# Two 576 KB weight transfers issued ahead of a 4 MB one at the head of a DMA queue

## The chip, the cores and the metric

The kernel runs on one core of a Trainium2 chip. The metric is the device time of one execution in microseconds. The core has five engines with instruction streams of their own: TensorE (PE in the profile, its weight loads PEld), VectorE (DVE), ScalarE (ACT), GpSimd (POOL) and SyncE (SP), and 16 DMA engines that carry the transfers that SP and ACT issue.

## The reference

One decoding step of a block with two branches over the same normalized input. The batch is 4, the model width D is 576, and there is one token per sequence.

```python
def reference(A_x, A_k_cache, A_v_cache, A_wq, A_wo, B_x, B_w1, B_w2, B_w3, B_w4):
    x = A_x                                   # (4, 1, 576)
    xn = _layernorm(x, axis=-1)
    return x + _A_ref(xn, A_k_cache, A_v_cache, A_wq, A_wo) + _B_ref(xn, B_w1, B_w2, B_w3, B_w4)

# branch A: attention over the last W = 2048 cached positions, 32 query heads, 16 KV heads, head size 128
    q = (x @ wq) split into heads
    p = softmax(q k^T * Dh ** -0.5);  o = p v
    return o @ wo
# branch B: mixer and MLP
    h = gelu(layernorm(x) @ w1)               # w1: 576 x 576
    hs = concatenate([g0, g1, g2, g3]) @ w2   # four shifted quarters of h; w2: 576 x 576
    x1 = x + hs
    return x1 + gelu(layernorm(x1) @ w3) @ w4 # w3: 576 x 4608, w4: 4608 x 576
```

With one token per sequence the shifts along the sequence leave only zeros in the shifted quarters, so the product with w2 is taken of an array of zeros (`hs_inT`), as the kernel has it.

## The kernel before

All weights and the window of the caches are read once from device memory: 88.49 MB. Nearly all of it goes over SP's queue, as the list `prog["sp"]`, which is sorted by each transfer's key (line 638) and issued in that order. A transfer that has to wait for a semaphore holds up all that SP would issue behind it.

At the head of that queue stand the weights of the first stages, each cut in a main part (rows 0 to 511, four rows on each of 128 partitions) and a rest (rows 512 to 575, split in halves over 128 partitions, `rag_src`, line 209). The keys set the order: wq and its rest (-50 and -49, lines 274 and 275), w1 main and rest (-48, line 276), w2 main and rest (-47, line 277), w3 main and rest (-46, line 278), the first 24 row groups of w4 (-45, line 281), then the 16 blocks of the K cache of 2 MB (lines 295 to 297), the 8 of V of 4 MB (lines 298 to 301) with the rest of w4 among them, and wo in five pieces (lines 304 to 307). The input x is issued on ACT's queue (line 273). The main parts of wq, w1 and w2 take 4096, 576 and 576 KB; their rests take 512, 72 and 72 KB.

Some buffers are used twice, and this sets waits. The main part of wq lies in the third and fourth slot of the K ring (line 88), so the third K transfer waits until the query projection is done (`["q"]`, line 296); from the fifth on, a K transfer waits for the transposes of the block that had its slot. w1 and w2 lie in the first half of `ktb` (lines 102 to 105), which the K stage uses later.

TensorE works through its own list in order of keys: the transposes of the normalized x (`pe_xT`, lines 331 to 340), the query projection in five steps (`pe_q`, lines 364 to 376, matmuls on line 371), the transposes of q (line 384), the product with w1 (`pe_hh`, line 400, matmuls on line 405), the product with w2 in two halves (`pe_hs`, line 410, lines 413 and 414), the transpose of the third layer norm's result, three matmuls that set accumulators to zero (`pe_bank0`, line 359), the product with w3 (`pe_h2`, lines 445 and 451), and the first part of the product with w4 (`pe_MO`, line 398). Then come the 16 K blocks (transposes on line 507, scores on line 514), the softmax, the product with V (line 575) and the product with wo (line 398 again). VectorE runs the layer norms (`ln_ops`, line 314, its last step on line 324) and copies out of PSUM, also in order of keys: the copy of the transposed x for the projection (line 352) stands behind the second layer norm. GpSimd sets up masks and clears buffers, among them the second half of `ktb` (line 246).

A wait of an operation is written as a list of names; for a transfer, `add_dma` (line 198) returns the semaphore and the count to wait for. Each pair of a list given to `add_dma` is one transfer that adds 16 to that semaphore.

Of the kernel before, what the change touches and what calls it, by code (L numbers as in the profile page):

```python
# [37 lines left out]
def bass_parallel_sum__sliding_block_cached__mixer_s_mlp__decode_kernel(  # L38
# [32 lines left out]
    with ExitStack() as ctx:  # L71
        def sb(name, shape, dt):
            return ctx.enter_context(nc.sbuf_tensor(name, shape, dt))

        def sem(name):
            return ctx.enter_context(nc.semaphore(name))
# [21 lines left out]
        def cut(n):  # L98
            nonlocal _o
            _o += n  # L100
            return ktb[:, _o - n:_o]
        w1main = cut(4 * D).rearrange("p (r n) -> p r n", r=4)
        w1rag = cut(HALF)
        w2main = cut(4 * D).rearrange("p (r n) -> p r n", r=4)
        w2rag = cut(HALF)
# [23 lines left out]
        hs_inT = sb("hs_inT", [128, 6, B], BF16)  # L129
# [64 lines left out]
        def add(engine, emit, waits=(), sig=None, key=0.0, inc=None):  # L194
            seqc[0] += 1
            prog[engine].append(Op(emit, waits, sig, key, seqc[0], inc))

        def add_dma(pairs, skey, waits=(), key=0.0, engine="sp"):
            if skey not in S:
                S[skey] = sem("s_" + "_".join(str(k) for k in (skey if isinstance(skey, tuple) else (skey,))))  # L200
            dma_count[skey] = dma_count.get(skey, 0) + 16 * len(pairs)

            def emit(e):
                for o_, i_ in pairs:
                    e.dma_start(o_, i_).then_inc(S[skey], 16)
            add(engine, emit, waits, None, key)
            return ("dma", skey, dma_count[skey])

        def rag_src(w_ap):
            return w_ap[512:576, :].rearrange("r (h n) -> (r h) n", h=2)  # L210
# [46 lines left out]
        for gl in range(2):  # L257
            for x in range(2 * NVS):
# [3 lines left out]
                  waits=["pick11"], sig=f"pick2{gl}{x}", key=-84 + 0.1 * (8 * gl + x))  # L262


        def mask_of(t, tag, view):
# [7 lines left out]
        ev_x = add_dma([(x_sb[:], x2)], "x", (), -100, engine="act")  # L273
        ev_wq = [add_dma([(kring[:, 2 * UE:4 * UE], A_wq[0:512, :].rearrange("(p r) n -> p (r n)", r=4))], "wq", (), -50),
                 add_dma([(wqrag, rag_src(A_wq))], "wqr", (), -49)]
        ev_w1 = add_dma([(w1main, B_w1[0:512, :].rearrange("(p r) n -> p r n", r=4)), (w1rag, rag_src(B_w1))], "w1", (), -48)
        ev_w2 = add_dma([(w2main, B_w2[0:512, :].rearrange("(p r) n -> p r n", r=4)), (w2rag, rag_src(B_w2))], "w2", (), -47)
        ev_w3 = add_dma([(vring[:, 0:4 * F], B_w3[0:512, :].rearrange("(p r) n -> p (r n)", r=4)), (w3rag, rag_src(B_w3))],
                        "w3", (), -46)
        w4s = B_w4.rearrange("(p r) n -> p r n", r=W4R)  # L280
# [69 lines left out]
        for idx, (src, tag, dst) in enumerate(((xn_bf, "ln1", xnT), (xn2_bf, "ln2", xn2T))):  # L350
            add("pe", pe_xT(src, idx), waits=["ident_bf", tag], sig=f"xT{idx}", key=-50 + idx)
            add("dve", lambda e, dst=dst, idx=idx: e.tensor_copy(out=dst[:], in_=XTps[idx]), waits=[f"xT{idx}"], sig=f"xnT{idx}",  # L352
                key=-29 + idx * 0.1)
# [36 lines left out]
        for k in range(2):  # L390
            for g in range(2):
# [3 lines left out]
                    waits=["qTp1"], sig=f"qT{2 * k + g}", key=-10 + 0.1 * k)  # L395
# [4 lines left out]
        def pe_hh(e):  # L400
# [4 lines left out]
                    ins = e.matmul(HHps[h], lhsT=x_, rhs=w, start=(r == 0), stop=(r == 4), tile_position=(0, 32 * h),  # L405
                                   skip_group_check=True)
            return ins
        add("pe", pe_hh, waits=[ev_w1, "xnT1"], sig="hT", key=-24)

        def pe_hs(h):  # L410
            def f(e):
                for r in range(4):
                    e.matmul(HSps, lhsT=hs_inT[:, r, :], rhs=w2main[:, r, HALF * h:HALF * (h + 1)], start=(r == 0), stop=False)
                return e.matmul(HSps, lhsT=hs_inT[:, 4 + h, :], rhs=w2rag, start=False, stop=True)
            return f
        for h in range(2):
            cs = slice(HALF * h, HALF * (h + 1))
            add("pe", pe_hs(h), waits=[ev_w2, "hs_inT"] + (["x1a"] if h else []), sig=f"hs{h}", key=-23 + h)
            add("dve", lambda e, cs=cs: e.tensor_tensor(out=x1_bf[:, cs], in0=HSps, in1=xn_bf[:, cs], op=ALU.add),
                waits=[f"hs{h}"], sig="x1" if h else "x1a", key=-7 + 0.1 * h)  # L420
        ln_ops(2, x1_bf, x1n_bf, ["x1"], "ln3", -6)
# [3 lines left out]
            waits=["hT", "ln3_sd"], sig="gelu_h", key=-5.9)  # L425
# [38 lines left out]
        for k in range(3):  # L464
            add("pe", pe_h2(k), waits=[ev_w3] + (["x1nT", "gelu_h", "h2_zero"] if k == 0 else []), sig=f"h2_{k}", key=-18 + k)
            add("act", lambda e, k=k: e.activation(out=h2_sb[:, k], in_=H2ps[k], func=ACTF.Gelu_apprx_tanh), waits=[f"h2_{k}"],
                sig=f"gelu2_{k}", key=-5 + 0.1 * k)
# [3 lines left out]
            waits=["h2Tp"], sig="h2T", key=-4.5)  # L471
# [16 lines left out]
        def evac(n):  # L488
            if n % 8 in ACT_EVAC:
                return "act", lambda e: e.activation(out=ktbuf[:, n % NKT], in_=tb[n % 4], func=ACTF.Copy)  # L490
            return "dve", lambda e: e.tensor_copy(out=ktbuf[:, n % NKT], in_=tb[n % 4])  # L491

        for n in range(NB):
            c, k = n // NBLK, n % NBLK
            if k == 0:
                add("dve", lambda e, c=c: e.tensor_copy(out=Qs[:, c % N_CB, :], in_=Qpad_t[:, 128 * (4 * CH[c][0] + CH[c][1]):][:, 0:128]),
                    waits=[f"SC{c - 2}"] if c >= 1 else ["qT3"], key=n)
            eng, f = evac(n)
# [11 lines left out]
        def emit_SC(e, k):  # L510
# [11 lines left out]
            waits=["rmax"], sig="negb", key=KS + 0.05)  # L522
        for q in range(4):
            add("act", lambda e, q=q: e.activation(out=P_sb[:, q, :], in_=Sps[:, q, :], func=ACTF.Exp,
                                                   bias=negb[:, 0:1], scale=scale, accum_out=rs4[:, q:q + 1]),
                waits=["negb"], sig=f"exp{q}", key=KS + 0.1 + 0.01 * q)
# [16 lines left out]
        for qt in range(4):  # L543
            k0 = KS + 0.9 + 0.1 * qt
            add("pe2", pe_PT(qt), waits=[f"PTx{q}" for q in range(4)] + (["pick217"] + [f"E{NB - 1 - k}" for k in range(4)] if qt == 0 else []),
                sig=f"PTp{qt}", key=k0)
            if qt % 2 == 1:
                add("dve", lambda e, qt=qt: e.tensor_copy(out=PT_t[:, 512 * qt:512 * (qt + 1)], in_=ps[:, 4 + qt, :]),
                    waits=[f"PTp{qt}"], sig=f"PT{qt}", key=k0)
            else:  # L550
                add("act", lambda e, qt=qt: e.activation(out=PT_t[:, 512 * qt:512 * (qt + 1)], in_=ps[:, 4 + qt, :], func=ACTF.Copy),
                    waits=[f"PTp{qt}"], sig=f"PT{qt}", key=k0)
# [3 lines left out]
            waits=["rinv", "ident_f"], sig="diag", key=KS + 0.82)  # L556
        add("pe2", lambda e: e.matmul(rinvps, lhsT=ones_f[:], rhs=diag[:], start=True, stop=True),
            waits=["diag", "ones_f", "PT1"], sig="rinvp", key=KV + 0.5)
        add("dve", lambda e: e.tensor_copy(out=rinvB[:].rearrange("p (c u e) -> p c u e", u=NU, e=2),
                                           in_=rinvps.rearrange("p (u c e) -> p c u e", u=NU, e=2)),  # L560
            waits=["rinvp"], sig="rinvB", key=KV - 2)
# [29 lines left out]
        for bp in range(NPAIR):  # L591
            k0 = KV + 2 * NVS * (bp + 1) - 0.5
            add("dve", lambda e: e.tensor_scalar(out=tmp[:], in0=ps[:, 0, 128:256], scalar1=maskd[:, 1:2], scalar2=None, op0=ALU.mult),  # L593
                waits=[f"PV{2 * NVS * (bp + 1) - 1}", "maskd"], sig=f"F{bp}", key=k0)
# [4 lines left out]
                waits=["rinvB", f"fold{bp}"], sig=f"O{bp}", key=k0 + (3 if bp == 0 else 0.2))  # L599
# [5 lines left out]
            waits=["OR"], sig="ORT", key=KE + 0.3)  # L605
# [137 lines left out]
```

## Time and profile before

| | |
|---|---|
| median of 3 runs | 214.57 us (214.45 to 214.62) |
| the profiled execution | 214.63 us |
| its span (first to last instruction) | 213.4 us |
| busy: TensorE / VectorE / ScalarE / GpSimd | 170.5 / 119.2 / 61.1 / 16.4 us |
| read from device memory | 88.49 MB, 415 GB/s over the span |
| mean granted TensorE clock | 0.959 |

The profile is of one execution. Its times count from the span's start, and 1.2 us of the execution lie around the span. A row of the timeline gives start, duration, engine, line, operation and, in brackets, the idle time ahead of it with what ended it. "SPq" rows are the instructions by which SP issues transfers. In a row of stretches, the columns after the stretch are its length, the busy time of PE, PEld, DVE, ACT and POOL with the count of instructions, the granted TensorE clock, the mean busy share of the 16 DMA engines, and GB/s. Short stretches can show a share over 1.

### The profile page before, as it was taken

The page shows a single profiled execution, that of the slowest core. Times are in us where ns is not written, and L with a number is a line of the kernel's source. Part 1 is how long each engine was busy: PE and PEld are TensorE (multiplying, and loading weights), DVE is VectorE, ACT ScalarE, POOL GpSimd, SP SyncE. Part 2 cuts the span into 40 slices and gives each one's busy share as a digit, 9 for nine tenths or more (in the row PEclk, how much of TensorE's full clock was granted, in tenths as well). Part 3 has the DMA queues.
Part 4 walks back from the last instruction along what each step waited for, and adds up shares of the span by engine and source line. Part 5 has one row for each costly group of instructions (what it writes and reads, how often), then busy time and mean ns, then how long its engine had stood idle before and what let it go on. Part 6 is the DMA issues. An engine that isn't in the chain of part 4 may idle for free.

```text
span 213.4 us, 4862 instructions
## 1 busy us (share of the span) xinstructions
PE 170.5 (80%) x2207; PEld 131.1 (61%) x2211; DVE 119.2 (56%) x172; ACT 61.1 (29%) x72; POOL 16.4 (8%) x39
## 2 busy tenths in 40 slices
PE   2028377699999999999999923899999868599965
PEld 0013125368877888777888811598888658488732
DVE  4973700037767777776676766999675573600110
ACT  2001302026655666665556645100000000000000
POOL 8992000000000000000000000000000000000000
PEclk9999859699999999999999995999999999999999
DMA  7999989999999999999999999999999999999992
GB/s 290 399 386 495 442 366 437 420 427 428 424 421 430 433 424 427 433 430 421 428 433 458 412 455 418 433 436 421 436 430 427 436 424 436 405 430 420 433 414 101
DMA packets 5794, 88.65 MB, mean 415 GB/s; under 512 B 652, under 2 KB 1048, under 8 KB 1816
## 3 DMA queue, kind: packets, MB, share of 16 engines
q1 hardware_dynamic: 5768, 88.49, 97.5%
q8 instruction: 8, 0.13, 0.2%
q10 hardware_dynamic: 16, 0.01, 0.0%
q14 instruction: 2, 0.02, 0.0%
HBM read 88.49 MB, written 0.00 MB: 415 GB/s over the span
## 4 chain that ended last, share of the span: by engine, by line
DMA 65%; PE 23%; DVE 9%; ACT 1%; issue 1%; SPq 0%
DMA kring<-in_A_k_cache_dram 39%; DMA vring<-in_A_wo_dram 13%; DMA vring<-in_A_v_cache_dram 12%; PE ps L575 10%; PE ps L507 7%; DVE xn_bf L324 4%; PE ps L514 2%; PE ps L371 2%; DVE vring L542 1%; DVE rmax L520 1%; DVE ktb L567 1%; PE ps L536 1%; DMA x_sb<-in_A_x_dram 1%; ACT ktb L490 0%; DVE stats L315 0%
## 5 line engine op out<-in xcount | busy, mean ns | idle before, releaser
L491 DVE COPY ktb<-ps 128x1024 bf16<-128x1024 bf16 x80 | 53.8, 690 | 23.7 <-PE ps L507 23.3
L507 PEld LDWEIGHTS ps<-perm_bf,kring 128*128 128x128 bf16 x1024 | 57.3, 98 | 10.8 <-issue 8.1
L507 PE MATMUL ps<-perm_bf,kring 128*128 128x128 bf16 x1024 | 62.5, 219 | 1.3 <-DMA kring<-in_A_k_cache_dram 0.6
L490 ACT ACTIVATE ktb<-ps 128x1024 bf16<-128x1024 bf16 x48 | 49.0, 1023 | 30.8 <-PE ps L507 30.0
L567 DVE TENSOR_TENSOR ktb<-PT,mH_bf 128x4096 bf16<-128x4096 bf16 x16 | 36.2, 2288 | 12.8 <-PE ps L575 12.8
L575 PE MATMUL ps<-vring,ktb 128*128 128x256 bf16 x256 | 28.6, 273 | 4.1 <-DMA vring<-in_A_v_cache_dram 2.3
L575 PE MATMUL ps<-kring,ktb 128*128 128x256 bf16 x256 | 28.6, 273 | 2.6 <-DMA kring<-in_A_v_cache_dram 2.6
L575 PEld LDWEIGHTS ps<-vring,ktb 128*128 128x128 bf16 x256 | 24.9, 98 | 7.5 <-issue 3.4
L575 PEld LDWEIGHTS ps<-kring,ktb 128*128 128x128 bf16 x256 | 25.0, 98 | 6.1 <-issue 2.8
L634 ACT ACTIVATE out_sb<-ps 4x288 bf16<-4x288 f32 x1 | 0.4, 401 | 76.2 <-PE ps L398 76.2
L514 PE MATMUL ps<-ktb,Qs 128*32 128x512 bf16 x272 | 17.8, 382 | 1.2 <-ACT ktb L490 1.2
L335 PE MATMUL ps<-ident_bf,xn_bf 4*128 4x4 bf16 x8 | 0.6, 170 | 11.9 <-DVE xnT L352 9.4
L593 DVE TENSOR_SCALAR tmp<-ps,maskd 128x128 f32<-128x128 f32 x2 | 0.7, 351 | 16.5 <-PE ps L575 16.5
L514 PEld LDWEIGHTS ps<-ktb,Qs 128*32 128x32 bf16 x272 | 5.7, 95 | 6.7 <-DVE ktb L491 1.4
L536 PE MATMUL ps<-vring,pick_bf 128*32 128x256 bf16 x64 | 3.9, 411 | 6.4 <-DVE rinv L554 6.4
L398 PE MATMUL ps<-vring,h2T_sb 128*4 128x288 bf16 x72 | 6.3, 337 | 2.8 <-DMA vring<-in_B_w_dram 2.8
L335 PEld LDWEIGHTS ps<-ident_bf,xn_bf 4*128 4x128 bf16 x8 | 0.4, 112 | 12.8 <-DVE xnT L352 9.5
L324 DVE TENSOR_SCALAR xn_bf<-xn_bf,mv,rstd 4x576 bf16<-4x576 bf16 x1 | 7.9, 7889 | 0.0
L536 PEld LDWEIGHTS ps<-vring,pick_bf 128*32 128x32 bf16 x64 | 2.1, 121 | 8.1 <-DVE rinv L554 6.9
L246 POOL MEMSET ktb<- 128x8192 bf16 x1 | 6.9, 6924 | 0.0
L398 PEld LDWEIGHTS ps<-vring,h2T_sb 128*4 128x4 bf16 x72 | 3.4, 97 | 5.5 <-DMA vring<-in_B_w_dram 3.0
L398 PE MATMUL ps<-vring,ORT 128*4 128x288 bf16 x64 | 4.6, 286 | 2.4 <-DMA vring<-in_A_wo_dram 2.2
(115 smaller groups left out, 85.0 us busy)
## 6 DMA issues: line engine op xcount, KB each, us to landing
kring<-in_A_k_cache_dram SPq DMA_DIRECT2D x16, 2048.0 KB, 14.7
vring<-in_A_v_cache_dram SPq DMA_DIRECT2D x4, 4096.0 KB, 24.6
kring<-in_A_v_cache_dram SPq DMA_DIRECT2D x3, 4096.0 KB, 33.9
vring<-in_B_w_dram SPq DMA_DIRECT2D x1, 4608.0 KB, 25.0
kring<-in_A_wq_dram SPq DMA_DIRECT2D x1, 4096.0 KB, 12.5
kring<-in_A_v_cache_dram SPq DMA_DIRECT2D x2, 2048.0 KB, 27.2
vring<-in_B_w_dram SPq DMA_DIRECT2D x1, 3456.0 KB, 34.5
vring<-in_A_wo_dram SPq DMA_DIRECT2D x1, 1872.0 KB, 30.4
```

What stands on the lines that cost most here:

```text
L246: P(lambda e: e.memset(ktb[:, NKT // 2 * 1024:NKT * 1024], 0.0), key=-92, inc=(("E", LB - 2), 1))
L324: add("dve", lambda e: e.tensor_scalar(out=dst[:], in0=src[:], scalar1=mv[:, idx, 0:1], scalar2=rstd[:, idx:idx + 1], op0=ALU.subtract, op ...
L371: ins = e.matmul(Qps[k // 4][32 * j:32 * j + B], lhsT=x_, rhs=w, start=False, stop=(r == 4), tile_position=(0, 32 * j), skip_group_check=True)
L398: return e.matmul(ACC[h], lhsT=lhsT, rhs=rhs, start=start, stop=stop, tile_position=(0, 32 * h), skip_group_check=True)
L490: return "act", lambda e: e.activation(out=ktbuf[:, n % NKT], in_=tb[n % 4], func=ACTF.Copy)
L491: return "dve", lambda e: e.tensor_copy(out=ktbuf[:, n % NKT], in_=tb[n % 4])
L507: ins = e.transpose(tb[j % 4][:, t, :], kslot_t(k)[:, 8 * kb + t, :], perm_bf[:])
L514: ins = e.matmul(Sps[32 * u:32 * u + 32, q, :].rearrange("p (t i) -> p t i", t=16), lhsT=Qs[:, k, 32 * u:32 * u + 32], rhs=ktgrp[:, (4 * k ...
L520: add("dve", lambda e: e.tensor_reduce(out=rmax[:], in_=Sps, axis=AX.XY, op=ALU.max), waits=["SCend"], sig="rmax", key=KS)
L536: ins = e.matmul(ps[32 * j:32 * j + 32, 4 + qt, 256 * ih:256 * (ih + 1)].rearrange("p (t a e) -> p t a e", a=NPAIR, e=2), lhsT=pick_bf[:, ...
L567: return lambda e: e.tensor_tensor(out=PTpad[:, n % 4], in0=PTv[:, qt, NH * h:NH * (h + 1), bp, :].unsqueeze(2).to_broadcast([128, NH, NX, ...
L575: ins = e.matmul(ps[:, 0, 0:256], lhsT=PTpad[:, 2 * (k % 2) + h, 2 * g:2 * g + 2].rearrange("p t h e -> p (t h e)"), rhs=vslot(k)[:, Dh * ...
```

## The change

The transfers of the main parts of w1 and w2 get keys of their own, -52 and -51, and so stand ahead of wq in SP's queue. The rests keep their places. Each main part and each rest has a semaphore of its own now, and the products with w1 and w2 wait for two each. The bytes, the sizes of the transfers and their number are the same.

```diff
-        ev_w1 = add_dma([(w1main, B_w1[0:512, :].rearrange("(p r) n -> p r n", r=4)), (w1rag, rag_src(B_w1))], "w1", (), -48)
-        ev_w2 = add_dma([(w2main, B_w2[0:512, :].rearrange("(p r) n -> p r n", r=4)), (w2rag, rag_src(B_w2))], "w2", (), -47)
+        ev_w1 = [add_dma([(w1main, B_w1[0:512, :].rearrange("(p r) n -> p r n", r=4))], "w1", (), -52),
+                 add_dma([(w1rag, rag_src(B_w1))], "w1r", (), -48)]
+        ev_w2 = [add_dma([(w2main, B_w2[0:512, :].rearrange("(p r) n -> p r n", r=4))], "w2", (), -51),
+                 add_dma([(w2rag, rag_src(B_w2))], "w2r", (), -47)]
...
-        add("pe", pe_hh, waits=[ev_w1, "xnT1"], sig="hT", key=-24)
+        add("pe", pe_hh, waits=ev_w1 + ["xnT1"], sig="hT", key=-24)
...
-            add("pe", pe_hs(h), waits=[ev_w2, "hs_inT"] + (["x1a"] if h else []), sig=f"hs{h}", key=-23 + h)
+            add("pe", pe_hs(h), waits=ev_w2 + ["hs_inT"] + (["x1a"] if h else []), sig=f"hs{h}", key=-23 + h)
```

## Prediction

> **What bounds the kernel now.** I read the page first: the span, the DMA row of the 40 slices, the queues, and the chain that ended last.
>
> ```profile
> span 213.4 us, 4862 instructions
> ...
> DMA  7999989999999999999999999999999999999992
> ...
> q1 hardware_dynamic: 5768, 88.49, 97.5%
> q8 instruction: 8, 0.13, 0.2%
> ...
> DMA 65%; PE 23%; DVE 9%; ACT 1%; issue 1%; SPq 0%
> ```
>
> One queue (SP's, q1) carries 88.49 MB, and its packets fill 97.5% of 16 DMA engines over the whole span. The slices show no hole between the first and the last. The chain is mostly transfers too, but its shares say little here: it follows waits, and a wait on a transfer that sits in a full queue is not the cause of the transfer's lateness. So I asked for stretches, to see at what rate the queue runs at each stage (the last two columns are the DMA share and GB/s).
>
> ```profile
> 0.00:2.00 2.00, 0.62 (x2) 0.13 (x2) 0.00 (x0) 0.59 (x1) 1.34 (x8) 1.00 0.55 150
> ...
> 1.50:1.80 0.30, 0.30 (x2) 0.01 (x1) 0.00 (x0) 0.30 (x1) 0.27 (x2) 1.00 0.06 8
> ...
> 2.00:13.30 11.30, 0.74 (x7) 0.26 (x6) 10.09 (x12) 1.09 (x3) 11.09 (x12) 1.00 0.91 380
> ...
> 14.60:18.00 3.40, 3.38 (x38) 1.33 (x42) 0.17 (x1) 0.00 (x0) 2.75 (x16) 1.00 1.08 438
> 18.00:30.00 12.00, 6.16 (x57) 2.34 (x45) 5.44 (x20) 2.88 (x5) 0.00 (x0) 0.80 1.00 430
> ...
> 59.40:123.00 63.60, 62.67 (x1040) 50.86 (x1040) 44.67 (x79) 39.59 (x39) 0.00 (x0) 1.00 1.01 431
> ...
> 184.00:210.80 26.80, 22.01 (x219) 16.53 (x221) 3.74 (x6) 0.00 (x0) 0.00 (x0) 1.00 0.95 399
> 210.80:213.40 2.60, 0.66 (x8) 0.26 (x8) 0.45 (x1) 0.40 (x1) 0.00 (x0) 0.91 0.01 2
> ```
>
> The kernel is a queue that starts at 1.8 us, runs at 430 to 438 GB/s without a break and ends at 210.8 us, with 2.6 us of tail. An edit moves the end only if it changes the bytes, the rate, the start or the tail, or if it makes the queue run empty. The bytes do not change.
>
> **The change, part by part.** Next come SP's own instructions in the timeline (start, duration), and the sizes and times to landing of its transfers.
>
> ```profile
> 0.80 0.41 SPq L205 DMA_DIRECT2D kring<-in_A_wq_dram  x1
> 1.27 0.41 SPq L205 DMA_DIRECT2D PT<-in_A_wq_dram  x1
> 1.73 2.04 SPq L205 DMA_DIRECT2D ktb<-in_B_w_dram  x4
> 3.81 0.45 SPq L205 DMA_DIRECT2D vring<-in_B_w_dram  x1
> ...
> 49.59 10.04 SPq L205 DMA_DIRECT2D kring<-in_A_k_cache_dram  x3
> ```
>
> ```profile
> kring<-in_A_k_cache_dram SPq DMA_DIRECT2D x16, 2048.0 KB, 14.7
> ...
> kring<-in_A_wq_dram SPq DMA_DIRECT2D x1, 4096.0 KB, 12.5
> ...
> ktb<-in_B_w_dram SPq DMA_DIRECT2D x3, 576.0 KB, 14.5
> ...
> PT<-in_A_wq_dram SPq DMA_DIRECT2D x1, 512.0 KB, 13.3
> ...
> ktb<-in_B_w_dram SPq DMA_DIRECT2D x2, 72.0 KB, 14.3
> ```
>
> *Moved: two issues and 1.18 MB.* SP issues four instructions for w1 and w2 (2.04 us, 0.51 each) behind the two of wq. Afterwards the two of 576 KB stand first; wq, the rest of wq and the two of 72 KB follow. There are six issues in either order, so the w3 transfer that starts issuing at 3.81 still does so, within 0.1 us, and everything behind it on SP (w4, the K transfers) too. Nothing is moved past POOL's queue, and x comes over ACT's queue.
>
> *wq lands later.* Before, it lands at 0.80 + 12.5 = 13.3 and its rest at 1.27 + 13.3 = 14.6. Two transfers of 576 KB are 1.18 MB; at the 431 GB/s of the steady stretch that is 2.7 us, so 16.0 and 17.3 after. Who waits? TensorE's query projection (L371), and what TensorE has queued behind it: the transposes of q, the products with w1 and w2, the third layer norm's transpose, and the product with w3 (L445).
>
> ```profile
> 6.29 7.89 DVE L324 TENSOR_SCALAR xn_bf<-xn_bf,mv,rstd 4x576 bf16<-4x576 bf16 x1
> ...
> 14.90 3.58 PE L371 MATMUL ps<-kring,xnT 128*4 128x512 bf16 x32
> ...
> 20.27 0.78 PE L405 MATMUL ps<-ktb,xn2T 128*4 128x288 bf16 x10
> ...
> 27.49 1.14 PE L359 MATMUL ps<-zeros_bf 128*128 128x384 bf16 x3
> ...
> 30.18 1.51 PE L445 MATMUL ps<-vring,x1nT 128*4 128x384 bf16 x16 [1.55 <-DMA ktb<-in_B_w_dram]
> ...
> 39.41 4.47 PE L398 MATMUL ps<-vring,h2T_sb 128*4 128x288 bf16 x48 [2.82 <-DMA vring<-in_B_w_dram]
> ...
> 44.72 1.34 PEld L507 LDWEIGHTS ps<-perm_bf,kring 128*128 128x128 bf16 x24 [0.37 <-issue]
> ```
>
> The projection starts at 14.9 in the trace, not at 13.3: it waits for the transposed x, which VectorE copies only behind its 7.89 us instruction. So of the 2.7 us only 16.0 - 14.9 = 1.1 us is new delay. That hides in the next idle stretch: L445 sat 1.55 us until the last of w3 landed at 30.18, and that landing stays, because the bytes ahead of it are the same. If this cover were gone (a delay over 1.55 us), the next is the 2.82 us before L398, which waits for w4. Together they cover 4.4 us against 1.1.
>
> *The early landing.* w1 and w2 are first read at 20.27, by when all four transfers had landed before as well (issued from 1.73 on, 14.3 to 14.5 to landing). TensorE runs its program in order and still takes the projection first. Earlier w1 starts nothing earlier: gain zero.
>
> *The K transfers.* The third K slot lies on wq, so SP issues it when the projection is done. This is where a delay could reach the queue; the chain shows it.
>
> ```profile
> 14.97 3.97 PE ps L371 x30
> 18.94 0.02 issue
> 18.96 0.54 SPq L205
> 19.50 0.04 issue
> 19.54 39.90 DMA kring<-in_A_k_cache_dram
> 59.44 0.05 issue
> ```
>
> Issued at 18.96, it and the next land by 59.44: about 40 us of older transfers lie ahead, while the same kind takes 14.7 us when three are in flight. Issuing at 20.1 instead removes 1.1 from a reserve of over 25 us. The next K issue, at 49.59, hangs on TensorE at 44.72 and so on w4, which does not move; it still has 59.44 - 49.59 = 9.9 us of queue ahead of it. Cost zero.
>
> *Added waits.* TensorE waits for two semaphores ahead of L405 and two ahead of the first product with w2, one more each. Behind them stands TensorE's whole program, but everything waited for has landed at about 18 us (as before: the sum of bytes up to the last rest is the same) and the readers come at 20.27 or later. The trace shows no wait that finds its semaphore high; the nearest rows are the 0.02 to 0.05 us "issue" pieces of the chain, so 0 to 0.1 us together, inside the 1.55. I take 0.
>
> *A different first transfer.* This is the one part for which the trace shows no row. The queue's head now consists of two 576 KB transfers instead of one of 4 MB. Up to 1.8 us next to nothing moves (8 GB/s from 1.5 on). From 0 to 13.3 the first two stretches give 150 x 2.0 + 380 x 11.3 = 4594 KB, which at 431 GB/s takes 10.7 us; so at most 0.8 us of the 11.5 us from 1.8 on is ramp. If small transfers fill the 16 engines faster, this is the most they can give back: -0.8. From the other side, every transfer takes 1.0 us from issue (0.80) to bytes (1.8); two short ones at the head that each exposed this once would cost 2 x 1.0 = 2.0 us. I take 0, by the nearest row: 14.6 to 18.0 is just the stretch of the w1 and w2 transfers, and with its queue filled it ran at 438 GB/s, no slower than the steady 431.
>
> The Trainium skill says otherwise about small transfers. "DMA: Bandwidth & Descriptors", section "Anatomy of one DMA", fits one transfer to 2.0 us plus its bytes over 436 GB/s, and its section "Bandwidth" asks for 1 MiB or more per transfer; taken in series, two at the head would by that estimate add 2 x 2.0 = 4 us. The stretch at 438 GB/s speaks against a price in series once transfers are queued; no row here shows the head itself.
>
> **Sum.** Against the profiled execution: 213.4 us of span, + 0 (landing of wq) + 0 (K) + 0 (waits) + 0 (head) = 213.4, and the 1.2 us that lie around the span (that execution took 214.63): 214.6 us. The median of the runs shown is 214.57, so this is no change.
>
> **Rivals.**
>
> *The head runs dry (slower).* Place: the first 5 us of SP's queue. If each 576 KB transfer is done before the next one's bytes come, the engines idle for up to 1.0 us, twice: 214.6 + 2.0 = 216.6; half of it gives 215.6. It decides from the point where SP's interval between issues (0.46 us, 0.80 to 1.27) exceeds a transfer's own time (590 KB at 431 GB/s, 1.37 us). The rows stand against it by a factor of three; for it speaks only that no row shows the start with small transfers. The skill's fixed 2.0 us is this rival's rule. Chance 0.12.
>
> *The ramp shortens (faster).* Up to 0.8 us: 213.8 at best, 214.1 for a typical 0.5. For it speaks the 0.91 share and 380 GB/s of the first stretch against 431 later; against it, that a ramp is mostly the time until first bytes, which both orders pay. Chance 0.17.
>
> *The engines end less evenly (slower).* In the last 26.8 us the share falls to 0.95 and the rate to 399 GB/s: some engines are done while others still work (5% of 26.8 is 1.3 us on average). The end is that of the last engine. Instruction fetches ride on the same engines: 8 packets, 0.2% of 16 x 213.4 us, or some 0.85 us each. Another order could put a second one on the last engine: 215.5. Against it: the program of each engine hardly changes. Chance 0.08.
>
> *It does nothing that can be measured.* This is the forecast. The share of the time that the edit touches is covered twice. Chance 0.63.
>
> **How the numbers follow.** Forecast 214.6. About 0.2% (0.43 us) is what a measurement of this kernel can tell from no change. Within it: 0.63. Faster by more: 0.17, the shortened ramp. Slower by more: 0.12 + 0.08 = 0.20. The range for 8 in 10 reaches from 213.9, nearly the whole ramp, to 215.6, half of the dry head and the whole uneven end; what is left out is the full dry head and little else. The likeliest case alone holds 214.2 to 215.0.
>
> **What would show it.** In the changed kernel's profile: wq's time to landing grows to about 14 us from a later issue (near 1.8), so it lands near 16; the projection (L371) starts near 16 instead of 14.9; L445 still starts near 30.2, with idle time ahead of it near 0.4 instead of 1.55; L398 still near 39.4; the K issues at 49.6 and the 59.4 landing stand; DMA shares of 8 or 9 from the second slice on. I am wrong if the rate in the first 5 us differs by more than a few hundred KB, if L398 or the first K landing moves by over 0.4 us, or if the last transfer's landing shifts against the stretches before it.

## The result and the profile after

The changed kernel takes 214.93 us (median of 22 runs, 214.25 to 215.35) against 214.51 us of the kernel before (22 runs, 214.34 to 214.77). The ratio is 1.0015 with a 95% interval of 1.0009 to 1.0021. So it is slower by some 0.3 to 0.4 us: clear of zero, and just within the 0.43 us that the forecast called no change. The spread says more than the median: 1.1 us after, 0.43 us before.

The page of the changed kernel has the same bytes and the same full queue:

```profile
span 213.6 us, 4863 instructions
...
DMA  7989999999999999999999999999999999999992
...
q1 hardware_dynamic: 5768, 88.49, 97.4%
```

The profiled execution took 214.92 us, 0.29 more than the one of before. Where that enters is read from its timeline (start, duration; the added lines move L371 to L373, L445 to L447, L398 to L400):

```profile
0.80 0.87 SPq L205 DMA_DIRECT2D ktb<-in_B_w_dram  x2
...
1.73 0.42 SPq L205 DMA_DIRECT2D kring<-in_A_wq_dram  x1
...
16.40 3.58 PE L373 MATMUL ps<-kring,xnT 128*4 128x512 bf16 x32 [1.44 <-DMA kring<-in_A_wq_dram]
...
29.15 1.14 PE L361 MATMUL ps<-zeros_bf 128*128 128x384 bf16 x3
...
30.42 0.12 PEld L447 LDWEIGHTS ps<-vring,x1nT 128*4 128x4 bf16 x8 [0.83 <-DMA ktb<-in_B_w_dram]
...
39.26 3.10 PE L400 MATMUL ps<-vring,h2T_sb 128*4 128x288 bf16 x48 [2.38 <-DMA vring<-in_B_w_dram]
...
49.10 11.08 SPq L205 DMA_DIRECT2D kring<-in_A_k_cache_dram  x3
```

and from the chain (start, length):

```profile
1.73 14.63 DMA kring<-in_A_wq_dram
16.36 0.04 issue
16.40 4.20 PE ps L373 x39
...
21.20 38.45 DMA kring<-in_A_k_cache_dram
59.64 0.05 issue
...
185.61 25.34 DMA vring<-in_A_wo_dram
210.96 0.04 issue
```

wq lands at 16.36, 0.3 us later than the 16.0 that its extra bytes account for. The last of w3, which has the same bytes ahead of it as before, lands 0.24 us later (30.42 against 30.18), the fourth K transfer 0.20 later (59.64 against 59.44), and wo 0.19 later (185.61 + 25.34 = 210.95 against 183.76 + 27.00 = 210.76). The offset is there by 16 us and is then carried to the end. These are one trace each, and single executions differ by as much: a kernel below whose head is that of before lands w3 at 29.92, in an execution of 214.39 us. So the place of the offset is read from the head itself. TensorE, late by 1.66 us ahead of L447 (29.15 against 27.49), is on time again at L400.

What happens in the head is seen when the DMA row is asked for a stretch of 1.2 us at the change from w2 to wq, cut in 40 slices of 30 ns. One 32 KB packet in a slice reads 1092 GB/s there, since 32,768 bytes in 30 ns are that. A row counts a packet in the slice in which it starts. The 154 more in some slices are each one of the last five 4.6 KB packets of w2; the 16 packets under 512 B are 4-byte writes to its semaphore.

```profile
GB/s 1246 1246 3431 0 1246 1093 2338 1092 1092 0 1092 0 1092 0 0 0 1092 0 0 0 0 1092 0 0 0 0 0 0 0 0 0 0 0 0 0 1092 0 0 0 0
DMA packets 37, 0.55 MB, mean 456 GB/s; under 512 B 16, under 2 KB 16, under 8 KB 21
```

The stretch runs from 4.96 to 6.16 us. The first packets of wq on 13 of the 16 engines start by 5.35; the last three start near 5.45, 5.6 and 6.0. Read packet by packet, an engine as a rule starts its next transfer 6 ns after its semaphore write. Four writes, from 5.06 to 5.11, are followed by nothing at once, and the four first packets of wq that follow no write start at 5.16, 5.45, 5.59 and 6.01: so three engines stood idle for 0.3 to 0.95 us (the pairing is inferred, since the profile does not name the engines). Their first packets were slow as well, 2.08, 1.91 and 1.43 us where all but one of the others took 1.21 to 1.34. wq has landed when all 16 engines have written its semaphore, so three late ones are enough.

### The profile page after: what moved, and what is told of

It reads as the page before. It is cut to its first block, busy times and chain, and to the rows that moved or that the text cites. A ratio compares the mean times of both kernels' runs of the same rounds, so it can differ in the third digit from the quotient of the medians.

```text
span 213.6 us, 4863 instructions
## 1 busy us (share of the span) xinstructions
PE 171.6 (80%) x2207; PEld 131.7 (62%) x2211; DVE 119.3 (56%) x172; ACT 61.2 (29%) x72; POOL 16.4 (8%) x39
## 4 chain that ended last, share of the span: by engine, by line
DMA 69%; PE 24%; DVE 4%; ACT 1%; SPq 1%; issue 1%
DMA kring<-in_A_k_cache_dram 39%; DMA vring<-in_A_wo_dram 12%; DMA vring<-in_A_v_cache_dram 12%; PE ps L577 11%; PE ps L509 7%; DMA kring<-in_A_wq_dram 7%; PE ps L516 2%; PE ps L373 2%; DVE vring L544 1%; DVE rmax L522 1%; DVE ktb L569 1%; PE ps L538 1%; SPq L205 1%; ACT ktb L492 0%; ACT Qpad L526 0%
## 5 line engine op out<-in xcount | busy, mean ns | idle before, releaser
L577 PE MATMUL ps<-vring,ktb 128*128 128x256 bf16 x256 | 30.3, 282 | 3.9 <-DMA vring<-in_A_v_cache_dram 2.3
L577 PEld LDWEIGHTS ps<-vring,ktb 128*128 128x128 bf16 x256 | 25.7, 101 | 8.1 <-issue 3.2
L595 DVE TENSOR_SCALAR tmp<-ps,maskd 128x128 f32<-128x128 f32 x2 | 0.7, 350 | 14.8 <-PE ps L577 14.8
L400 PE MATMUL ps<-vring,h2T_sb 128*4 128x288 bf16 x72 | 4.9, 286 | 2.4 <-DMA vring<-in_B_w_dram 2.4
L400 PE MATMUL ps<-vring,ORT 128*4 128x288 bf16 x64 | 4.6, 286 | 2.4 <-DMA vring<-in_A_wo_dram 2.2
L400 PEld LDWEIGHTS ps<-vring,h2T_sb 128*4 128x4 bf16 x72 | 2.9, 84 | 4.1 <-DMA vring<-in_B_w_dram 2.5
## 6 DMA issues: line engine op xcount, KB each, us to landing
kring<-in_A_wq_dram SPq DMA_DIRECT2D x1, 4096.0 KB, 14.6
```

Of the source, the lines that this page charges most:

```text
L400: return e.matmul(ACC[h], lhsT=lhsT, rhs=rhs, start=start, stop=stop, tile_position=(0, 32 * h), skip_group_check=True)
L577: ins = e.matmul(ps[:, 0, 0:256], lhsT=PTpad[:, 2 * (k % 2) + h, 2 * g:2 * g + 2].rearrange("p t h e -> p (t h e)"), rhs=vslot(k)[:, Dh * ...
```

## The experiments

The theory after this reading: at the head of the queue single engines get their first packet of wq late, and the latest engine carries that to the end. The rivals: the change from short to long transfers costs this wherever it stands; the later projection holds up a K transfer; the two rests back to back, or the added waits, cost it. The first four kernels are edits of the changed kernel.

### One short transfer ahead

```diff
-        ev_w2 = [add_dma([(w2main, ...)], "w2", (), -51),
+        ev_w2 = [add_dma([(w2main, ...)], "w2", (), -47.5),
```

> Only the main part of w1 stands ahead of wq; w2 goes back behind. Theory head (the queue's stock is thin in the first microseconds, so that single engines get their first packet of wq late at the change from short transfers to wq, and the latest engine carries this to the end): one short transfer ahead, stock thin as well; an offset between 0 and the changed kernel's 0.3 us against before, and wq landing 1.4 to 2.0 us later than the 13.3 of before. Rival changeover (a change from short to long transfers costs this wherever it stands): 0.3 us, as there is one such change ahead of wq here too. Rival projection (the later query projection holds up a K transfer): wq lands only 1.4 us later, hidden behind the 1.6 us until the transposed x is there, so 0. Rival rests (the two rests of w1 and w2 back to back cost it): 0, they are apart again.

Measured: 214.06 us (213.92 to 214.19, 11 runs), ratio 0.998, interval 0.9971 to 0.9989. It is faster than the kernel before by 0.45 us, which none of these theories had; the shortened ramp among the prediction's rivals did. The DMA row from 3.4 to 4.6 us, same slices of 30 ns:

```profile
GB/s 0 1707 307 614 307 307 307 307 2339 3431 2185 2185 154 2185 2185 1092 0 0 1092 0 0 0 0 0 0 0 0 0 0 0 0 0 0 0 0 0 0 0 0 0
```

No engine is late: the last first packet of wq starts near 3.95, half a microsecond after the first, and the idle time of the 16 engines there adds up to 0.07 us. And the queue is ahead of the one before, as the landing of w3 and of wo show:

```profile
29.68 0.10 PEld L447 LDWEIGHTS ps<-vring,x1nT 128*4 128x4 bf16 x8 [1.33 <-DMA ktb<-in_B_w_dram]
```

```profile
184.98 25.29 DMA vring<-in_A_wo_dram
```

w3 lands 0.50 us earlier than before (29.68 against 30.18), wo 0.49 earlier (210.27 against 210.76). So there is a gain in a short transfer at the head, and in the changed kernel it is hidden under a loss. The change from short to long transfers, which is here too, costs nothing that shows; that rival falls.

Part of the gain shows in the head of the kernel before, from 1.7 to 2.9 us:

```profile
GB/s 0 77 0 39 1092 3277 1092 0 1092 3315 1092 0 0 0 1092 0 0 2185 0 1092 0 0 0 0 0 1092 0 0 1092 0 0 0 0 0 0 0 0 0 0 0
q1 hardware_dynamic: 16, 0.52, 152.8%
```

The 16 first packets of wq start from 1.83 to 2.55, and they take 1.83 us each on average (152.8% of 1.2 us). The next 16, from 3.6 to 4.8 us, take 1.24 (103.1%). With w1 ahead the engines start no sooner, but the slow beginning falls on packets of 4.6 KB, and the first packets of wq take 1.28 us. That this is the whole gain is not shown.

### A long transfer first

```diff
+        wq_s = A_wq[0:512, :].rearrange("(p r) n -> p r n", r=4)
+        ev_wqa = add_dma([(wqmain[:, 0:2, :], wq_s[:, 0:2, :])], "wqa", (), -53)
-        ev_wq = [add_dma([(kring[:, 2 * UE:4 * UE], ...)], "wq", (), -50),
+        ev_wq = [add_dma([(wqmain[:, 2:4, :], wq_s[:, 2:4, :])], "wq", (), -50),
...
-            add("pe", pe_q(r), waits=[ev_wq[r // 4], "xnT0"], ...
+            add("pe", pe_q(r), waits=[ev_wqa, ev_wq[r // 4], "xnT0"], ...
```

> wq's main part goes in two transfers of 2 MB: the first half, then w1 and w2, then the second half; the projection waits for both, so it is as late as in the changed kernel. Theory head: the first half gives 5 us of work at once, so the stock is there; no engine is late at the second half, wq lands 2.7 to 2.8 us later than before (near 16.0) and the time is that of before, within 0.1 us. Rival changeover: the change from w2 to the second half costs the same 0.3 us, with late first packets near 10.5 us. Rival projection: 0.3 us, since the projection starts near 16.1. Rival rests: 0.3 us.

Measured: 214.51 us (214.34 to 214.69, 11 runs), ratio 1.0, interval 0.9991 to 1.0009. The projection is as late as expected, the third K transfer is issued at 20.62 as in the changed kernel (18.96 before), and nothing comes of it:

```profile
16.14 3.58 PE L375 MATMUL ps<-kring,xnT 128*4 128x512 bf16 x32 [1.17 <-issue]
```

The two rests are back to back here too. The rivals of the projection and of the rests fall, and so does the second change from short to long.

### The rests first

```diff
-        ev_w1 = [add_dma([(w1main, ...)], "w1", (), -52), add_dma([(w1rag, ...)], "w1r", (), -48)]
-        ev_w2 = [add_dma([(w2main, ...)], "w2", (), -51), add_dma([(w2rag, ...)], "w2r", (), -47)]
+        ev_w1 = [add_dma([(w1main, ...)], "w1", (), -48), add_dma([(w1rag, ...)], "w1r", (), -52)]
+        ev_w2 = [add_dma([(w2main, ...)], "w2", (), -47), add_dma([(w2rag, ...)], "w2r", (), -51)]
```

> The two rests of w1 and w2 (72 KB each, some 0.2 us of transfer) stand ahead of wq, and the main parts go back behind. Theory head: transfers far shorter than SP's 0.46 us between issues; the engines run dry twice, wq starts late by the time that two issues and their way to the engines take, 0.5 to 2 us, and the end is later by as much. Rival changeover: 0.3 us. Rival projection: wq lands under 1 us later and the projection still waits for the transposed x, so 0. Rival rests: the two stand back to back, 0.3 us.

Measured: 215.06 us (214.93 to 215.51, 7 runs), ratio 1.0032, interval 1.0021 to 1.0043, at the low end of what was expected. SP issues wq at the same moment as in the changed kernel, and the engines now wait for it. From 2.6 to 3.8 us:

```profile
1.72 0.42 SPq L205 DMA_DIRECT2D kring<-in_A_wq_dram  x1
```

```profile
GB/s 192 231 269 230 135 77 1150 58 39 1131 1112 0 1092 2185 1092 0 3277 1092 1092 0 0 0 0 0 0 0 1092 0 0 1092 1092 0 1092 0 0 0 0 0 0 0
```

The first packets of wq start from 2.8 to 3.6, which is 1.1 to 1.9 us after the issue at 1.72; before, on idle engines, they start 1.0 to 1.75 us after it. Only 3 to 7 of the 16 engines are at work between 2.75 and 3.05. This is the head run dry as the prediction described it, at a price of some 0.55 us where it put up to 1.0 us, twice. In the changed kernel wq is issued at 1.73, and its packets should by this have been there at 3.6, long before 5.1, when they are wanted. So the late engines of the changed kernel are another thing than a queue that is plainly empty.

### The head of before, the rest of the change

```diff
-        ev_w1 = [..., "w1", (), -52), ..., "w1r", (), -48)]
-        ev_w2 = [..., "w2", (), -51), ..., "w2r", (), -47)]
+        ev_w1 = [..., "w1", (), -48), ..., "w1r", (), -46.8)]
+        ev_w2 = [..., "w2", (), -47), ..., "w2r", (), -46.7)]
```

> The head is that of before (wq and its rest first); behind it w1, w2 and then the two rests back to back, with the semaphores and waits of the changed kernel. Theory head: the time of before within 0.1 us, since nothing short stands ahead. Rival changeover: the time of before. Rival projection: the time of before. Rival rests (and that of the two added waits): 0.3 us slower than before.

Measured: 214.50 us (214.28 to 214.81, 11 runs), ratio 1.0003, interval 0.9994 to 1.0012. The new semaphores, the added waits and the grouped rests cost nothing that shows. (The projection is not late here and w1 is not early.)

### The changed kernel again

No edit. The question is whether the late engines make its times.

> The changed kernel once more, for a second trace of its head. Theory head: the loss sits at the change to wq again, on a few engines, of a size that varies from run to run (its times spread over 1.1 us, those of before over 0.4): late first packets of wq after 5.0 us, the last of w3 landing between 29.7 and 30.5. Rival (the first trace showed a chance event): no late first packets and yet 214.9 us.

Measured: 214.95 us (214.19 to 215.27, 11 runs), ratio 1.0016, interval 1.0006 to 1.0026. The profiled execution was one of its best, 214.21 us. Its stretch from 4.96 to 6.16 us, and its landings of w3 and wo:

```profile
GB/s 154 1553 461 154 461 2492 0 3277 3431 1092 2338 2185 0 154 0 0 0 1092 0 1092 0 0 0 0 0 0 0 0 0 0 0 0 0 0 0 0 0 0 0 0
```

```profile
29.71 0.10 PEld L447 LDWEIGHTS ps<-vring,x1nT 128*4 128x4 bf16 x8 [1.10 <-DMA ktb<-in_B_w_dram]
```

```profile
184.87 25.48 DMA vring<-in_A_wo_dram
```

The same kernel, this time with all first packets by 5.55, and the last two of them on engines that were at work on w2 until then: w3 lands 0.71 us earlier than in the first trace (29.71 against 30.42), wo 0.60 earlier (210.35 against 210.95), and the execution is 0.71 shorter (214.21 against 214.92). So an execution without late engines came near the time of the kernel with w1 alone ahead. By the times alone, most executions are not of this kind; the slowest loses 1.1 us against the fastest.

### What makes the engines late: five more

These were to tell apart the bytes ahead of wq, its packets' size, its place in the queue, and the stock ahead of it.

Two halves of w1 ahead, 288 KB each (an edit of the kernel with w1 alone ahead):

```diff
-        ev_w1 = [add_dma([(w1main, ...)], "w1", (), -52),
+        w1s = B_w1[0:512, :].rearrange("(p r) n -> p r n", r=4)
+        ev_w1 = [add_dma([(w1main[:, 0:2, :], w1s[:, 0:2, :])], "w1", (), -52),
+                 add_dma([(w1main[:, 2:4, :], w1s[:, 2:4, :])], "w1b", (), -51),
```

> As with w1 alone ahead, but w1's main part goes in two transfers of 288 KB: the same bytes ahead of wq and the same time at the change to wq (near 3.5 us), but two transfers as in the changed kernel. If the number of transfers ahead makes the dry place: late first packets of wq, and 0.3 to 0.8 us slower than with w1 alone (214.4 to 214.9). If the bytes or the time ahead make it: 214.1 as with w1 alone.

Measured: 216.27 us (215.91 to 216.85, 5 runs), ratio 1.0085, interval 1.0072 to 1.0098; more than either side expected. From 3.6 to 6.0 us, in slices of 60 ns, where one 32 KB packet reads 546:

```profile
GB/s 1007 777 777 700 585 39 0 0 0 0 546 0 0 0 0 0 0 0 0 0 0 1092 546 546 0 1092 0 1638 0 546 546 1092 546 0 0 546 0 0 0 0
```

Most of the engines are late here: between 3.95 and 4.85 us a single packet starts. By the pairing of packets as above, 11 of the 16 stood idle, and eight of their first packets then took 1.5 to 1.7 us. w3 lands 2.2 us later than before:

```profile
32.37 0.10 PEld L449 LDWEIGHTS ps<-vring,x1nT 128*4 128x4 bf16 x8 [3.02 <-DMA ktb<-in_B_w_dram]
```

The same bytes ahead of wq in one transfer gained 0.45 us; in two they lose 1.75.

Half of w1 alone ahead (the second half goes behind wq, key -48.5 in place of -51 in the edit above):

> Only the first half of w1's main part (288 KB, one transfer) ahead of wq, the second half behind wq. wq is the second transfer, as with w1 alone, but its stock ahead is half as long: the 288 KB are done near 2.9 us. If the number of transfers ahead decides: 214.1 as with w1 alone. If it is the stock ahead (the engines go dry before wq's packets reach them): first packets of wq late by up to 1 us, 214.5 to 215.5.

Measured: 214.31 us (214.13 to 214.48, 11 runs), ratio 0.9993, interval 0.9984 to 1.0002. From 2.8 to 4.0 us:

```profile
GB/s 461 384 384 1476 384 231 3354 4523 1169 1246 0 2185 1169 1092 0 0 2185 0 0 0 0 0 0 0 0 0 0 0 0 0 0 0 0 0 0 0 0 0 0 0
```

With half of the stock and one transfer ahead, no engine is late by more than some 0.2 us; the two last start near 3.3. So a short stock does not make the engines late by itself. The gain is smaller than with the whole of w1 ahead, 0.20 us against 0.45, and its interval reaches zero.

w1 ahead on SP's queue, w2 on ACT's:

```diff
-        ev_w2 = [add_dma([(w2main, ...)], "w2", (), -51),
+        ev_w2 = [add_dma([(w2main, ...)], "w2", (), -51, engine="act"),
```

> w1 ahead of wq on SP's queue as with w1 alone, and w2's main part issued on ACT's queue behind x. The bytes early in the engines are those of the changed kernel, but wq is the second transfer of its queue and is issued 0.46 us earlier. If the late engines come from wq being the third transfer of its queue behind two short ones: none late, 214.0 to 214.2. If they come from 1.18 MB of short packets early in the engines, whatever queue: late ones as in the changed kernel, 214.7 to 215.1.

Measured: 214.22 us (214.03 to 214.38, 11 runs), ratio 0.9988, interval 0.9979 to 0.9997. None of the loss is there, and the spread is 0.35 us. But the early bytes of the changed kernel are not there either, against what the expectation took for granted. From 3.4 to 4.6 us, where the first packets of wq start, all packets are those of SP's queue:

```profile
DMA packets 58, 0.64 MB, mean 537 GB/s; under 512 B 16, under 2 KB 16, under 8 KB 42
...
q1 hardware_dynamic: 58, 0.64, 135.1%
```

Of the 128 packets of w2 none starts before 4.6 us and three before 5; the rest come one by one between those of wq until 15.6. So this kernel repeats the head of the one with w1 alone ahead, and does not tell the early bytes from the place in the queue.

wq in two halves of 2 MB behind w1 and w2 (16 KB packets):

```diff
+        ev_wqa = add_dma([(wqmain[:, 0:2, :], wq_s[:, 0:2, :])], "wqa", (), -50.5)
```

> The changed kernel with wq's main part as two transfers of 2 MB (16 KB packets instead of 32 KB). If the long packets make the late start at the change to wq: none late, 214.1 to 214.3. If it is the engines' supply at that time, whatever comes: late first packets again, 214.7 to 215.1.

Measured: 215.37 us (214.81 to 215.43, 5 runs), ratio 1.0039, interval 1.0026 to 1.0052. This is above what was expected. In its trace, of the fastest of the five, two or three engines at a time stand idle between 5.1 and 5.8 us. So it isn't the 32 KB packets; with 16 KB (and one transfer more in the queue) the loss is rather larger.

Three short transfers ahead:

```diff
-                 add_dma([(wqrag, rag_src(A_wq))], "wqr", (), -49)]
+                 add_dma([(wqrag, rag_src(A_wq))], "wqr", (), -50.5)]
```

> w1, w2 and the 512 KB rest of wq ahead of wq's main part: three short transfers, the change to wq near 6.2 us instead of 5.0. If thin stock in the first microseconds makes the dry place, it is no deeper than in the changed kernel: 214.5 to 214.9. If each further short transfer ahead adds to it: over 215.1, with first packets of wq later than 1 us after the others. wq's main part lands near 17.5 and the projection starts there, still hidden by the 2.8 us ahead of the product with w4.

Measured: 214.70 us (214.04 to 215.12, 12 runs), ratio 1.0002, interval 0.9991 to 1.0013: inconclusive on the median. The spread of 1.1 us is that of the changed kernel, which suggests the loss in some executions; the traced one, of 214.54 us, has next to no idle time at the change to wq's main part. A third short transfer does not deepen the loss. The product with w3 starts only at 33.13 in this trace, behind the late projection and 2.95 us later than before, at no cost to the end that shows.

## Why the prediction was right, and where it was not

*What bounds the kernel.* Right: the queue. The offset of the head, 0.24 us at w3, is 0.19 at wo; 0.71 between two executions of one kernel is 0.60 at wo and 0.71 in the time.

*wq lands later, and the cover ahead of w3.* Right in kind: the delay of the projection (1.5 us where 1.1 was worked out) and of what follows it was absorbed. With the first half of wq in front a delay of 1.2 us cost nothing, and with three transfers ahead even the start of the product with w3 went back by 2.95 us at no cost that shows.

*The K transfers, the early landing, the added waits.* Right at zero each. For the waits the kernel with the head of before shows it (1.0003, interval 0.9994 to 1.0012), for the K transfers the one with half of wq first (1.0, interval 0.9991 to 1.0009), in which the third is issued as late as in the changed kernel. For the early landing it is read from the trace: the product with w1 starts behind the projection, at 21.93 where it started at 20.27.

*A different first transfer, taken as 0.* This is the term that was mis-sized. It is not nothing but the sum of two effects of opposite signs, both among the rivals. One is the cheaper start: a gain of 0.45 us when it stands alone (w1 only), inside the 0.8 us that the prediction worked out as its limit. The other is the late engines, up to 1.1 us, by the times in most executions but not in all. In the changed kernel they leave +0.3 to +0.4. That the sum stayed within 0.43 us of zero is luck in this term: the prediction put both aside, and neither is zero.

The row that I put in place of the head, the stretch from 14.6 to 18.0 us at 438 GB/s, shows short transfers in a queue that has long been full. It could not show this.

*The dry head.* Its place was right, its condition wrong. It was to decide when SP's interval between issues exceeds a transfer's own time. That happens with the rests first, and costs 0.55 us there. In the changed kernel the interval is a third of the transfer's time, and engines were late all the same. What the runs show as the condition: wq can be late when it is the third transfer of SP's queue behind two short ones (the changed kernel, two halves of w1, wq in halves), and was not when it is the second (w1 alone, half of w1, w2 on ACT's queue), nor when a long one stands first. The sharpest pair is w1 whole and in halves: the same bytes ahead, 214.06 and 216.27 us. Added up over the 16 engines from the packets' times, the idle time at the change to wq is 14.8 us with the two halves, 1.9 in the first trace of the changed kernel, 1.2 with wq in halves, 0.15 in the good execution of the changed kernel, and 0.44 or less with one short transfer ahead and with three. Why the third is late stays open. The profile has no record of what passes between SP's issue and an engine's first packet. In the second place wq was issued at 1.27 us and in the third at 1.73, and no run here told the place from the time of the issue.

The Trainium skill's fixed 2.0 us per transfer ("DMA: Bandwidth & Descriptors", section "Anatomy of one DMA"), taken in series, gives the wrong sign for one transfer of 576 KB ahead (-0.45 us), and is above what two of 288 KB cost (+1.75 against 4.0). The Trainium skill's page fits it to single transfers that GpSimd issues, and those here are issued by SP.

*The uneven end.* The share in the last stretch is 0.93:

```profile
184.00:211.10 27.10, 23.70 (x236) 17.81 (x237) 4.39 (x7) 0.00 (x0) 0.00 (x0) 1.00 0.93 392
```

Over the same stretch the kernel before shows 0.93 too, at 395 GB/s, since its transfers end earlier in it. Counted over the 26.76 us up to each execution's own last landing, the share is 0.95 before, 0.93 here, and 0.96 both in the good execution of the changed kernel and in the kernel with the head of before. So the engines end somewhat less evenly, as that rival had it, in the execution whose engines were late in the head and not in the good one. The mechanism that the rival named is not seen: the page of either kernel has 8 instruction packets (q8), none of them before 30 us and one after 207.

The kernel with w1 alone ahead beats both: 214.06 us, 0.2% under the kernel before.

## What to carry to other kernels

In a kernel that is one full queue from start to end, an order can cost nothing behind a long first transfer and still cost at the head: look at when the 16 first packets of each of the first three transfers start, in slices of some 30 ns, since the slowest engine sets the landing, and most of its lateness came through to the end here (2.2 us at w3 and 1.75 in the time, with two halves of w1). One short transfer first gained here and two lost, so try both. With the second on another queue the gain stayed (214.22 us), but its packets came late, one between two of the long ones. When times spread more after a change than before, compare a good and a bad execution of the same kernel before building on the median.

## What else the runs showed of the hardware

SP's issue of a transfer, 0.41 to 0.54 us in most rows, can take much longer in the first 8 us. In the kernel with two halves of w1 ahead the issue of w3 took 1.93 us, and in the one with half of w1 ahead that of w4 took 3.09:

```profile
4.43 1.93 SPq L205 DMA_DIRECT2D vring<-in_B_w_dram  x1
```

```profile
5.26 3.09 SPq L205 DMA_DIRECT2D vring<-in_B_w_dram  x1
```

In the second it delayed the K transfers' issue to 8.39 us, with the queue full, and cost nothing that shows. Whether the long issues and the late engines have one cause was not tried.

A 32 KB packet that is the first on an idle engine is slow: 1.83 us on average at the head of the kernel before and 1.77 with the rests first, against 1.21 to 1.24 for most packets once the queue is full. An engine that stood idle so lost more than its idle time.
